# A long convolution with a gated feed-forward: real and imaginary rows in partition halves, the K spectrum moved into the middle loop, feed-forward in chunk pairs

## The chip, the cores and the metric

The kernel runs on 1 core of one Trainium2 chip. The metric is the device time of one execution in microseconds (us). The kernel before takes 271.25 us (median of 40 runs, 269.36 to 272.9). Each run is counted fast or slow; on one core, slow means only more than 1.5% above the fastest run of the same kernel. Medians and ranges below are over all runs, ratios over the fast runs alone.

Engine names as the profile has them: PE is TensorE, PEld its weight loads, DVE is VectorE, ACT is ScalarE, POOL is GpSimd, SP is SyncE.

## The reference

```python
def ref_conv(q, k, v, shift_k, ssm_k, ssm_D):        # S = 2048, D = 640
    k_pad = jnp.pad(k, ((0, 0), (3, 0), (0, 0)))
    k_shift = sum(k_pad[:, t:t + S, :] * shift_k[:, 3 - t] for t in range(4))   # four taps
    kv = k_shift * v
    # y = causal convolution of kv with ssm_k: real FFT of length 2S = 4096, product, inverse
    y = irfft(rfft(pad(kv)) * rfft(pad(ssm_k)))[:, :S, :].astype(bf16)
    return q * (y + kv * ssm_D)

x  = A_q
xn = layernorm(x)
s  = ref_conv(xn, A_k, A_v, A_shift_k, A_ssm_k, A_ssm_D)
g  = silu(gelu(xn @ w1 + b1) @ w2 + b2)              # w1 is 640 x 1728, w2 is 1728 x 640
return x + s * g
```

(shortened: casts and the generation of the inputs are left out; the factor called q inside `ref_conv` is `xn`.)

The kernel makes the transforms out of matmuls. A first stage multiplies by the sine tables `WA` and `WB` (16 units for K, the filter, and 16 for U, the shifted k times v); its results go through scratch memory in DRAM (`scrK`, `scrU`), which transposes them. A second stage multiplies by a small matrix `F2m`. The spectra are multiplied; `I1a` and `I1b` are the first half of the inverse; its result goes through `scrC`; `GA` and `GB` finish it. The two feed-forward products (FFN1 with `w1`, FFN2 with `w2`) are fed to PE between these pieces. PSUM is the on-chip memory that the matmuls write, SBUF the one that holds the other tiles. An eviction below is a copy of a matmul result out of PSUM.

## The kernel before

First stage of K (its second stage then fills `Khat`, the whole K spectrum, in SBUF):

```python
def f1_unit(rhs, scr, n2, eng, ptag):
    o_sb = ep.tile([P, 2, D], BF16, tag="o" + ptag, bufs=3, name="f1o")
    for c, W in ((0, WA), (1, WB)):
        for h in range(2):                                   # 320 columns at a time
            hs = slice(h * HALF, (h + 1) * HALF)
            ps = ps_e.tile([P, 512], F32, tag=ptag, bufs=2, name="psf1")
            nc.tensor.matmul(out=ps[:, 0:HALF], lhsT=W[:, n2, :], rhs=rhs[:, hs], ...)
            evac(..., o_sb[:, c, hs], ps[:, 0:HALF])
    nc.gpsimd.dma_start(out=sv[:, :, n2, :], in_=o_sb[:])    # to scrK or scrU

def k_unit(n2):                                              # one K unit: transposes, copy, first stage
    tp = ps_e.tile([P, 1024], BF16, tag="tp", bufs=2, name="tpk")
    for t in range(DT):
        nc.tensor.transpose(out=tp[:, t * P:(t + 1) * P], in_=kf_v[:, t, n2, :], identity=ident[:])
    kT = ep.tile([P, D], BF16, tag="kT", bufs=2, name="kT")
    nc.scalar.copy(out=kT[:], in_=tp[:, 0:D])
    f1_unit(kT, scrK, n2, "act", "f1k")

# ... cut: f2k_unit, the same with F2m, into Khat ...
kv_unit(0)
for n2 in range(NJ):
    k_unit(n2)
    emit_ffn(1)
```

The middle loop transforms U twice (the second time with swapped halves, `F2s`) and makes two products:

```python
psU  = ...  # F2m x uin   (two matmuls of 320 columns)
psUs = ...  # F2s x uin   (two more)
nc.vector.tensor_tensor(out=halves(p1[:]), in0=psU[...],  in1=halves(Khat[:, g, :]), op=ALU.mult)
nc.vector.tensor_tensor(out=halves(p2[:]), in0=psUs[...], in1=halves(Khat[:, g, :]), op=ALU.mult)
# psC = I1a x p1 + I1b x p2 ; copied to c_sb ; stored to scrC
```

## Time and profile before

| kernel | median us (range, runs) | PE busy us | PE idle us in the span | first FFN1 matmul, us |
|---|---|---|---|---|
| before | 271.25 (269.36 to 272.9, 40) | 222.4 | 46.6 | 34.6 |

The idle time is the span of the profiled execution (269.1 us) less PE's busy time.

Lines of the profile page of the kernel before. The first line is PE's busy time and share; the two strips cut the span into 40 slices of 6.7 us, each digit a busy share in tenths; then two groups of instructions (busy time and mean ns of one), and one line of the DMA issues (size, median us from issue to landing).

```profile
PE 222.4 (83%) x1424; PEld 136.0 (51%) x1437; DVE 178.3 (66%) x348; ACT 163.8 (61%) x335; POOL 49.4 (18%) x77
PE   1038689999958889999999999999998999687960
PEclk9999999999979999999999999999999999999995
...
L481 ACT CAST c_sb<-psC 128x640 bf16<-128x640 f32 x32 | 22.1, 692 | 23.2 <-PE psC L480 15.4
...
L464 PE MATMUL psUs<-uin,F2s 128*128 128x320 bf16 x64 | 13.9, 299 | 0.2
...
scrK<-f1o POOLq DMA_DIRECT2D x16, 320.0 KB, 4.4
```

The first FFN1 matmul, in the timeline of PE (start, duration, engine, line, operation):

```profile
34.59 1.24 PE L251 MATMUL ps_299<-xnT,w_sb 128*128 128x512 bf16 x4
```

PE is the limit: thin in the first five slices, then busy for nine tenths of the time or nearly so until about 230 us. `psUs` is the second transform of U, which the change removes (its 13.9 us is a sum of overlapping durations; at the pitch of 0.136 us it is 8.7 us).

The same kernel by stretches: up to the first FFN1 matmul, feed-forward beside the K and U stages, middle loop, end, and what follows. Columns: stretch and its length, busy us (and instructions) of each engine, granted TensorE clock, share of the DMA engines' time, GB/s.

```profile
0.00:34.60 34.60, 13.26 (x78) 8.07 (x79) 23.87 (x72) 17.27 (x32) 9.68 (x21) 1.00 0.92 326
34.60:157.00 122.40, 115.03 (x721) 67.94 (x728) 81.64 (x164) 101.99 (x234) 23.97 (x32) 0.99 0.55 177
157.00:224.00 67.00, 63.45 (x427) 40.98 (x432) 51.84 (x73) 35.74 (x56) 10.71 (x15) 1.00 0.52 163
224.00:260.00 36.00, 30.48 (x201) 19.02 (x199) 18.38 (x36) 8.81 (x15) 4.00 (x7) 1.00 0.70 236
260.00:270.00 10.00, 0.24 (x2) 0.00 (x0) 2.55 (x5) 0.00 (x0) 1.08 (x2) 0.61 0.16 66
```

Nearly half of PE's 46.6 us of idle time, 21.3 us, lies before the first FFN1 matmul. So the time is this start, plus PE's work after it, plus small gaps, plus a tail.

### The profile page before, as it was taken

How to read it: one execution, taken by the hardware profiler on the slowest of the kernel's cores; microseconds unless marked ns; L12 is line 12 of the kernel's file. 1: busy time of each engine (PE TensorE's matmuls, PEld its weight loads, DVE VectorE, ACT ScalarE, POOL GpSimd, SP SyncE). 2: the span in 40 equal slices, each digit the busy share in tenths (PEclk: the TensorE clock that was granted, in tenths of full speed). 3: DMA queues.
4: the chain of work that ended last, by engine and by line, in shares of the span. 5: the costliest groups of instructions: out<-in, count | busy, mean ns of one | idle time of the engine just before them, and what ended most of it. 6: DMA issues, size and time to landing. Idle time of an engine off the chain costs nothing.

```text
span 269.1 us, 4113 instructions
## 1 busy us (share of the span) xinstructions
PE 222.4 (83%) x1424; PEld 136.0 (51%) x1437; DVE 178.3 (66%) x348; ACT 163.8 (61%) x335; POOL 49.4 (18%) x77
## 2 busy tenths in 40 slices
PE   1038689999958889999999999999998999687960
PEld 0024345557635544566654456775565554454730
DVE  2785999944469899998422047349898982366770
ACT  1268499999626999974699936237664647300200
POOL 4122312342401211121112101011222222011100
PEclk9999999999979999999999999999999999999995
DMA  4999996565456565724344285214656652889721
GB/s 64 354 416 393 391 370 234 174 197 241 158 184 191 174 212 166 240 97 132 103 136 122 97 268 174 97 49 138 203 159 188 192 198 100 226 267 380 258 85 54
DMA packets 27877, 53.03 MB, mean 197 GB/s; under 512 B 5645, under 2 KB 19666, under 8 KB 27857
## 3 DMA queue, kind: packets, MB, share of 16 engines
q1 hardware_dynamic: 23056, 33.11, 40.8%
q0 software_dynamic: 4800, 19.67, 18.4%
q8 instruction: 11, 0.18, 0.3%
q14 instruction: 10, 0.07, 0.1%
HBM read 34.41 MB, written 18.36 MB: 196 GB/s over the span
## 4 chain that ended last, share of the span: by engine, by line
PE 32%; issue 24%; DMA 14%; DVE 14%; POOL 7%; ACT 6%; SPq 1%; POOLq 0%; DVEq 0%; ACTq 0%
DMA xc<-in_A_q_dram 4%; DMA w_exp<-scrW 4%; DMA uin<-scrU 3%; POOL scrC L483 3%; DVE stats L226 2%; POOL rstd L231 2%; DVE f1o L85 2%; PE psf2k L401 2%; DMA scrW<-wT_sb 2%; DVE kvtmp L410 2%; DVE uc L411 2%; DMA khc<-in_A_k_dram 2%; DVE xn L234 1%; POOL out_dram L533 1%; ACT f1o L83 1%
## 5 line engine op out<-in xcount | busy, mean ns | idle before, releaser
L262 PEld LDWEIGHTS <-hT 128*128 128x128 bf16 x448 | 44.1, 99 | 20.6 <-issue 2.3
L251 PEld LDWEIGHTS <-w_sb 128*128 128x128 bf16 x280 | 27.1, 97 | 29.7 <-issue 7.9
L481 ACT CAST c_sb<-psC 128x640 bf16<-128x640 f32 x32 | 22.1, 692 | 23.2 <-PE psC L480 15.4
L402 ACT CAST Khat<-psf2k 128x320 bf16<-128x320 f32 x64 | 25.9, 477 | 2.1 <-PE psf2k L401 2.0
L385 POOL DMA_DIRECT2D scrU<-f1o x16 | 11.0, 690 | 65.6 <-ACT f1o L83 39.3
L483 POOL DMA_DIRECT2D scrC<-c_sb x16 | 11.4, 714 | 62.5 <-ACT c_sb L481 50.7
L390 PE MATMUL tpk<-ident,Khat 128*128 128x128 bf16 x80 | 10.1, 262 | 14.3 <-DVE Khat L373 14.0
L226 DVE BATCH_NORM_STATS2 stats<-xc 128x6 f32<-128x320 bf16 x32 | 14.2, 467 | 10.9 <-DMA xc<-in_A_q_dram 10.9
L411 DVE TENSOR_TENSOR uc<-uc,kvtmp 128x1280 bf16<-128x1280 bf16 x24 | 19.6, 816 | 0.3
L410 DVE TENSOR_TENSOR kvtmp<-khc,w_exp 128x1280 bf16<-128x1280 bf16 x24 | 19.6, 817 | 0.2
L401 PE MATMUL psf2k<-kin,F2m 128*128 128x320 bf16 x64 | 16.9, 311 | 2.8 <-DMA kin<-scrK 2.8
L390 PEld LDWEIGHTS <-Khat 128*128 128x128 bf16 x80 | 9.1, 154 | 17.8 <-DVE Khat L373 14.3
L266 DVE TENSOR_TENSOR xn<-xn,sl 128x320 bf16<-128x320 bf16 x32 | 10.1, 319 | 10.9 <-ACT sl L265 10.8
L385 POOL DMA_DIRECT2D scrK<-f1o x16 | 11.1, 695 | 31.7 <-ACT f1o L83 29.9
L461 PE MATMUL psU<-uin,F2m 128*128 128x320 bf16 x64 | 14.0, 300 | 1.4 <-DMA uin<-scrU 1.2
L464 PE MATMUL psUs<-uin,F2s 128*128 128x320 bf16 x64 | 13.9, 299 | 0.2
L519 PE MATMUL psY<-cab,GA 128*128 128x320 bf16 x32 | 9.1, 300 | 5.4 <-DMA cab<-scrC 4.7
L392 ACT COPY kT<-tpk 128x640 bf16<-128x640 bf16 x16 | 12.9, 813 | 0.0
L241 ACT COPY xnT<-tpx 128x512 bf16<-128x512 bf16 x20 | 11.2, 613 | 0.2 <-PE tpx L240 0.2
L240 PE MATMUL tpx<-ident,xn 128*128 128x128 bf16 x80 | 8.7, 234 | 2.9 <-DVE xn L234 2.5
L533 POOL DMA_DIRECT2D out_dram<-o_sb x8 | 4.4, 545 | 32.7 <-DVE o_sb L531 24.6
L401 PEld LDWEIGHTS <-F2m 128*128 128x128 bf16 x64 | 6.4, 101 | 7.5 <-issue 3.0
(679 smaller groups left out, 565.5 us busy)
## 6 DMA issues: line engine op xcount, KB each, us to landing
scrK<-f1o POOLq DMA_DIRECT2D x16, 320.0 KB, 4.4
scrU<-f1o POOLq DMA_DIRECT2D x16, 320.0 KB, 2.9
kin<-scrK SPq DMA_DIRECT2D x32, 160.0 KB, 2.6
uin<-scrU SPq DMA_DIRECT2D x16, 320.0 KB, 3.3
scrC<-c_sb POOLq DMA_DIRECT2D x16, 320.0 KB, 3.8
cab<-scrC SPq DMA_DIRECT2D x16, 320.0 KB, 5.2
khc<-in_A_k_dram SPq DMA_DIRECT2D x8, 320.0 KB, 3.5
vc<-in_A_v_dram SPq DMA_DIRECT2D x8, 320.0 KB, 3.7
```

The lines of the kernel that those rows point to most:

```text
L226: nc.vector.bn_stats(out=stats[:, j, h, :], in_=xc[:, j, h * HALF:(h + 1) * HALF])
L251: nc.tensor.matmul(out=ps[:, :], lhsT=w1_sb[:, t, ft * P:(ft + 1) * P], rhs=xnT[:, t, :], start=(t == 0), stop=(t == DT - 1))
L262: nc.tensor.matmul(out=ps[:, 0:HALF], lhsT=hT[0:M, ft, q * P:(q + 1) * P], rhs=w2_sb[0:M, ft, hs], start=(ft == 0), stop=(ft == FT - 1))
L385: nc.gpsimd.dma_start(out=sv[:, :, n2, :], in_=o_sb[:])
L390: nc.tensor.transpose(out=tp[:, t * P:(t + 1) * P], in_=kf_v[:, t, n2, :], identity=ident[:])
L401: nc.tensor.matmul(out=ps[:, 0:HALF], lhsT=F2m[:], rhs=kin[:, hs], start=True, stop=True)
L402: nc.scalar.copy(out=Khat[:, g, hs], in_=ps[:, 0:HALF])
L410: nc.vector.tensor_tensor(out=tmp[:], in0=khc[:, 3 - j:KR + 3 - j, :], in1=w_exp[:, j, :, :], op=ALU.mult)
L411: nc.vector.tensor_tensor(out=uc[:], in0=uc[:], in1=tmp[:], op=ALU.add)
L461: nc.tensor.matmul(out=psU[:, h, 0:HALF], lhsT=F2m[:], rhs=uin[:, h * HALF:(h + 1) * HALF], start=True, stop=True)
L481: nc.scalar.copy(out=halves(c_sb[:, g % 2, :]), in_=psC[:, :, 0:HALF])
L483: nc.gpsimd.dma_start(out=gC[g // 2], in_=c_sb[:])
```

## The change

The intent, in the words that came with it: "Real/imaginary rows in partition halves, one U transform with a half-swapped K copy, K second stage in the middle loop, FFN in chunk pairs, x and xn resident". With real and imaginary rows in halves of the partitions, exchanging them is a copy of 64 partitions. So K is exchanged once by two DMA transfers, in place of a second transform of every U group. In addition, `GA` and `GB` are computed by DVE and ACT instead of transposed from `WA` and `WB`, all K transposes come first, evictions are 640 wide, and the U evictions, before shared by DVE and ACT, all go to ACT.

The core of the diff (much is cut; moved code is shown as it is after):

```diff
+    def kt_unit(t):                       # K transposes: ten DVE copies of 1024 in place of 16 ACT copies
+        ... 
+            nc.vector.tensor_copy(out=kT[:, h * 8:(h + 1) * 8, t * P:(t + 1) * P], in_=tp[:])
     def f1_unit(rhs, scr, n2, engs, tag):
-        o_sb = ep.tile([P, 2, D], BF16, tag="o" + ptag, bufs=3, name="f1o")
+        o = ep.tile([P, 2, D], BF16, tag="f1o", bufs=3, name="f1o")
         for c, W in ((0, WA), (1, WB)):
+            ps = ps2("psf1")
             for h in range(2):
-                ... evac(..., o_sb[:, c, hs], ps[:, 0:HALF])            # 320 wide, four a unit
+                nc.tensor.matmul(out=ps[:, h, 0:H], lhsT=W[:, n2, :], rhs=rhs[:, h * H:(h + 1) * H], ...)
+            nc.scalar.copy(out=hv(o[:, c, :]), in_=ps[:, :, 0:H])       # 640 wide, two a unit
-    build_i2_by_transpose()               # GA, GB: 32 transposes and 4 ACT copies
+    wg_pair(GA, GB, fill_g)               # GA, GB: DVE products and masks, ACT sines
...
+    for t in range(DT):
+        kt_unit(t)
+    build_small_mats()                    # F2m, I1a, I1b (each with one sine on ACT)
+    wg_pair(GA, GB, fill_g)
+    emit_ffn(1)                           # first layer norm and its transposes
+    w2_sb = big.tile([P, FT, D], BF16, tag="w2", name="w2_sb")   # takes the place of the K filter
+    nc.sync.dma_start(out=w2_sb[...], in_=B_w2[...])             # about 2.1 MB, now just ahead of:
+    load_kv(8, 4)
+    load_kv(12, 4)
+    for n2 in range(NJ):
+        f1_unit(kT[:, n2, :], scrK, n2, "aa", "k")
+        ...
+        emit_ffn(1)
...
     # middle loop
-    psUs = F2s x uin; two products of 640
+    kk[0:64, :, 1, :] = kk[64:128, :, 0, :]; kk[64:128, :, 1, :] = kk[0:64, :, 0, :]   # two DMA
+    one product of 1280: psU (broadcast) x kk
```

## The prediction

> **What bounds it now.** TensorE. The page gives PE 83% busy, DVE 66%, ACT 61%. The view by stretches shows PE thin only in 0-34 us and 230-250 us; between, it is busy 8.4 to 10 of every 10 us. In steady stretches of the timeline a 512-column matmul costs 0.216 us (five in 1.08) and a 320-column one 0.136 us (fourteen in 1.91). At these rates PE streams 60.5 us of FFN1 (280), 61 us of FFN2 (448), 69.6 us of convolution matmuls (512), and 192 transposes. FFN1 starts at 34.6 us; about 207 us of PE work and 18 us of gaps follow, to 260 us; then a 9 us tail of DVE and the last store.
>
> **What the change does.**
> 1. The swapped-U matmul goes: 64 x 0.136 = 8.7 us of PE. The 32 table transposes go: about 3 us. All critical: -11.7 us.
> 2. Evictions: K transposes move from 16 ACT copies (0.81 us) to 10 DVE copies; first- and second-stage results leave PSUM 640 wide (0.69 us, as c_sb now) instead of 320 wide (0.43-0.48). ACT falls from 164 to about 153 us, which counts only in the K stage (ACT full, 40-70 us): 3 us per K unit becomes 2.
> 3. The two products per group become one of 1280 elements. The Trainium skill ("VectorE: DVE Perf Modes", Why PSUM operands drop a tier) says an fp32 PSUM operand allows only 1x; the trace agrees (640 elements 0.82 us, pitch 0.73). One product takes about 1.45 us: no gain.
> 4. Start: shift weights no longer go through DRAM (4.9 + 10.2 us in the chain); K filter and w1 load earlier. But DVE must do both table pairs (6 + 5 us), ten K copies (12), small matrices (6) and the first layer norm (7) before FFN1, which starts at about 37-41 us, no earlier than now, but with all K transposes and most of the K first stage behind it.
> 5. Middle loop: K second stage moves in (PE 0.27, ACT 0.69 us per group), plus two half-swap DMAs per pair (5.2 MB in all). With two K buffers the loop eviction 1.6 + swap 3-4 (160 KB loads from scrK take 2.6 now) + two products 2.9 us limits a group to about 2.1-2.3 us; PE needs 1.1 us plus FFN, 1.8 in all. DMA rises from 0.5 to about 0.8 of its limit. The loop takes 70-76 us against 67 now, gaps partly filled by FFN: 5-10 us given back.
> 6. End: x and xn stay resident (three 640 KB reloads gone), C rows are 2560 contiguous bytes, so the cab waits (4.7 us on PE) shrink; stores are single rows: tail 6 us instead of 9.
>
> **Sum.** PE work after FFN1 starts is about 183 us. 39 + 183 + 18 of gaps + 6 = 246 us span, 2 us more as time: **248 us**, range 236 to 262. Faster by over 2%: 0.88; within 2%: 0.08; slower: 0.04.
>
> **What would show it.** PE busy about 208 us; F2s matmuls gone; first FFN1 matmul at 37-41 us; K first stage at 2 us a unit with ACT full; one 1.4-1.5 us product per group; swapped K halves landing in 3-4 us, and products waiting for them; middle loop 70-76 us; PE waits for cab under 2 us; last matmul to end about 6 us.
>
> **What would make it wrong.** PE's fixed order puts convolution matmuls ahead of ready FFN work while a swap DMA is in flight, so that waits reach 20 us or more; DMA saturates in the middle loop; the shared two-slot PSUM pool (U, K, first stage, Y) serialises DVE and ACT; DVE load delays FFN1 beyond 45 us. In the other direction: FFN fills every gap and FFN1 starts at 33 us, 235 us.

## The result, and the profile after

| kernel | median us (range, runs) | PE busy us | PE idle us in the span | first FFN1 matmul, us |
|---|---|---|---|---|
| before | 271.25 (269.36 to 272.9, 40) | 222.4 | 46.6 | 34.6 |
| after | 272.11 (268.04 to 274.03, 20) | 216.5 | 52.4 | 56.2 |

Ratios here are the mean time of one kernel's fast runs over that of the other's of the same rounds, so they are not quite the ratios of the medians. After over before: 0.998 (95% interval 0.995 to 1.001); with the slow runs counted in, the ratio of the means is 1.003. The change did not move the time; 248 us and the range to 262 were wrong. PE lost 5.9 us of work and gained 5.8 us of idle time.

The page of the kernel after, the same kinds of lines:

```profile
PE 216.5 (81%) x1334; PEld 130.3 (48%) x1345; DVE 167.2 (62%) x300; ACT 157.9 (59%) x253; POOL 53.1 (20%) x91
PE   1648244489989999999988979879798998888970
PEclk9999955579999999999999999999999999999996
...
L465 ACT CAST c_sb<-psC 128x640 bf16<-128x640 f32 x32 | 22.4, 700 | 17.3 <-PE psC L464 15.3
...
scrK<-f1o POOLq DMA_DIRECT2D x16, 320.0 KB, 2.5
```

The first FFN1 matmul after:

```profile
56.18 1.38 PE L324 MATMUL ps_414<-xnT,w_sb 128*128 128x512 bf16 x4
```

By stretches, with the borders at the same events (first FFN1 matmul, start and end of the middle loop, end of PE's work):

```profile
0.00:56.20 56.20, 27.76 (x156) 17.39 (x157) 40.15 (x108) 29.21 (x38) 16.21 (x32) 0.79 0.82 298
56.20:140.00 83.80, 80.36 (x503) 48.12 (x507) 56.99 (x113) 62.23 (x105) 16.83 (x27) 1.00 0.33 121
140.00:222.00 82.00, 73.47 (x435) 41.74 (x439) 46.68 (x34) 60.33 (x98) 10.73 (x15) 1.00 0.81 243
222.00:260.40 38.40, 34.81 (x246) 23.01 (x244) 22.60 (x44) 5.65 (x13) 8.82 (x16) 1.00 0.59 210
260.40:269.00 8.60, 0.14 (x2) 0.00 (x0) 0.82 (x2) 0.44 (x1) 0.54 (x1) 0.75 0.05 19
```

From the first FFN1 matmul on, PE works 188.6 us and stands for 15.6 us (the differences of lengths and busy times in the three middle rows). PE's idle time before that matmul grew from 21.3 to 28.4 us; elsewhere it did not grow. The middle loop is longer (82 us against 67), but PE is busy in 73.5 us of it. So the question is the start. In the four slices from 27 to 54 us the strip of PE, which before reads 6, 8, 9, 9, now reads 2, 4, 4, 4, and in the last three of them the clock strip reads 5.

The stretch 20 to 60 us of the kernel after, in four windows:

```profile
20.00:30.00 10.00, 8.11 (x57) 5.82 (x56) 8.69 (x39) 5.30 (x8) 2.30 (x3) 1.00 1.00 389
30.00:40.00 10.00, 3.17 (x10) 1.26 (x10) 5.79 (x19) 5.89 (x8) 2.05 (x4) 0.63 0.74 266
40.00:50.00 10.00, 3.40 (x11) 1.25 (x10) 8.57 (x23) 5.04 (x8) 3.18 (x5) 0.50 0.78 264
50.00:60.00 10.00, 8.30 (x43) 4.94 (x44) 10.00 (x22) 8.67 (x15) 1.68 (x3) 0.68 0.40 164
```

From 30 to 50 us no compute engine is full (DVE comes nearest, 8.6 of 10 us from 40 to 50); PE does a third of what it could and ACT a half. That is the picture of engines waiting for one another or for transfers, not of too much work. The DMA engines are full from 20 to 30 us. Who waits is in the timeline of ACT of the kernel after (start, duration, engine, line, operation; in brackets the idle time before it and what ended it; L266 is the first-stage eviction, L163 and L167 the `GB` and `GA` sines, L232 the sine of a small matrix, L314 the copy of the transposed layer norm):

```profile
28.30 0.69 ACT L266 CAST f1o<-psf_453 128x640 bf16<-128x640 f32 x1
29.05 0.40 ACT L232 ACTIVATE k_all<-k_all,sin_bias 128x128 f32<-128x128 int32 x1
34.11 0.69 ACT L266 CAST f1o<-psf_466 128x640 bf16<-128x640 f32 x1 [4.65 <-DMA scrK<-f1o]
34.70 0.70 ACT L266 CAST f1o<-psf_470 128x640 bf16<-128x640 f32 x1
35.28 2.01 ACT L163 ACTIVATE GB<-qT,sin_bias 128x2048 bf16<-128x2048 int32 x1
...
37.75 0.42 ACT L232 ACTIVATE k_all<-k_all,sin_bias 128x128 f32<-128x128 int32 x1
...
49.69 0.69 ACT L266 CAST f1o<-psf_582 128x640 bf16<-128x640 f32 x1 [4.63 <-DMA scrK<-f1o]
...
53.74 1.08 ACT L314 COPY xnT<-tpx 128x512 bf16<-128x512 bf16 x2
```

ACT twice stands for 4.6 us at an eviction whose buffer is still being stored. Everything ACT does after it waits too. The Trainium skill ("TensorE: Matmul & The Clock Gate", Part 1) lists ScalarE's and VectorE's instruction queues as strict FIFO; the trace agrees: the sine at 37.75 us, whose input DVE had prepared by about 33 us, comes only after three evictions (34.11, 34.70 and 37.18 us) and the `GB` sine, and DVE in turn stands behind that sine. The timeline of DVE of the kernel after shows this (L298 is the first statistics instruction of the layer norm, which FFN1 needs):

```profile
32.79 1.21 DVE L166 TENSOR_SCALAR prodT<-prodT 128x2048 int32<-128x2048 int32 x1
38.21 0.29 DVE L235 TENSOR_TENSOR I1a<-k_all 128x128 bf16<-128x128 f32 x1 [4.21 <-ACT k_all L232]
...
38.95 0.49 DVE L298 BATCH_NORM_STATS2 stats<-xreg 128x6 f32<-128x320 bf16 x1
```

The stores that it all waits for are in the chain of waits that ended last, of the kernel after:

```profile
29.29 7.01 DMA scrK<-f1o
...
43.88 7.44 DMA scrK<-f1o
```

The median store of this kind lands in 2.5 us; these two took 7.0 and 7.4. They are not the only ones: the three stores issued from 26.9 to 29.3 us took 7.0 to 7.1 us and the three from 42.4 to 45.4 us 6.9 to 7.4 us. ACT's two long waits ended with the first store of each three (issued at 26.88 and 42.41 us, landed after 7.1 and 7.2 us). All six fell beside large loads: the `w2` load (2080 KB, issued at 24.8 us, landed after 13.1 us), then the last two loads of k and one of x (640 KB each, from 41.9 us). The Trainium skill ("DMA: Bandwidth & Descriptors", Issuing engines are not separate DMA queues) says that transfers issued by different engines run on the same 16 DMA engines and interleave. The traces agree with that reading: the stores are issued by POOL and the loads by SP, and yet the stores slow down. The experiments test it. All waits of ACT for K stores in the kernel after (total, times, longest):

```profile
ACT f1o L266 <- DMA scrK<-f1o: 9.7, 3, 4.7
```

A sum suggests why the change made this visible, and the old kernel did not mind. Slow stores as such are not new: in the kernel before, the first four K stores (issued from 22.6 to 35.7 us) fell beside its own `w2` load (issued at 18.7 us, landed after 18.9 us) and took 5.8 to 6.6 us. But the K units then came 2.5 to 6.3 us apart. With three buffers, a unit's store has the length of two further units to land in. Later, in its steady stretch, units were 2.48 us apart (from the times of the store issues), so a store had 5.0 us for its median of 4.4 us, and ACT waited for a K store only once in all, 1.4 us. After the change the units that ran unhindered are 1.2 us apart (issues at 26.88, 28.10 and 29.29 us), so a store has 2.4 us, just what an undisturbed one takes. This is an estimate from the two traces: the faster first stage used up the reserve of its own buffers.

PE, kept from work, also lost its clock. The timeline of PE of the kernel after, two first-stage pairs before and one after the long wait:

```profile
29.05 0.43 PE L263 MATMUL psf_470<-xreg,WB 128*128 128x320 bf16 x2 [0.16 <-ACT f1o L266]
34.85 0.69 PE L263 MATMUL psf_494<-xreg,WA 128*128 128x320 bf16 x2 [5.37 <-ACT f1o L266]
```

The pair takes 0.69 us instead of 0.43. The Trainium skill ("TensorE: Matmul & The Clock Gate", Part 1) lists two states of the clock gate, half and all pulses, and has it at half after an idle window of about 3.4 us. The trace agrees: after a wait of 5.37 us the granted clock is 0.50 in the window 40 to 50 us. Durations show the slow rate early on too, in both kernels: a single matmul of 320 columns took 0.43 to 0.47 us in the kernel before until 32.4 us and 0.30 us at 36.8 us, and 0.45 to 0.47 us in the kernel after up to 25 us. The clock column reads 1.00 in those stretches, so it can't be relied on there.

### The profile page after: what moved, and what is told of

Same layout as the page of the kernel before. It is cut to its first block, busy times and chain, and to the rows that moved or that the text cites. A ratio compares the mean times of both kernels' runs of the same rounds, so it can differ in the third digit from the quotient of the medians.

```text
span 268.9 us, 3786 instructions
## 1 busy us (share of the span) xinstructions
PE 216.5 (81%) x1334; PEld 130.3 (48%) x1345; DVE 167.2 (62%) x300; ACT 157.9 (59%) x253; POOL 53.1 (20%) x91
## 4 chain that ended last, share of the span: by engine, by line
issue 39%; PE 29%; DMA 12%; POOL 7%; ACT 7%; DVE 4%; SPq 0%; POOLq 0%; ACTq 0%
DMA scrK<-f1o 5%; ACT f1o L266 4%; POOL scrC L467 4%; DMA kf_sb<-in_A_ssm_k_dram 3%; DMA cab<-scrC 3%; POOL out_dram L347 2%; PE tpk L249 2%; DVE prodT L166 1%; ACT xnT L314 1%; DMA scrC<-c_sb 1%; DVE xreg L250 1%; DVE prodT L177 1%; PE ps_1283 L336 1%; PE ps_1135 L336 1%; PE ps_977 L336 1%
## 5 line engine op out<-in xcount | busy, mean ns | idle before, releaser
L340 DVE TENSOR_TENSOR xreg<-xreg,sl 128x320 bf16<-128x320 bf16 x32 | 10.1, 322 | 26.6 <-ACT sl L339 26.6
L416 ACT CAST kk<-psk 128x640 bf16<-128x640 f32 x32 | 20.9, 705 | 0.0
L286 DVE TENSOR_TENSOR tmp<-k_all,w_exp 128x1280 bf16<-128x1280 bf16 x24 | 19.5, 812 | 0.1
L287 DVE TENSOR_TENSOR acc<-acc,tmp 128x1280 bf16<-128x1280 bf16 x24 | 19.5, 812 | 0.1
L414 PE MATMUL psk<-kin,F2m 128*128 128x320 bf16 x64 | 13.7, 298 | 6.6 <-DVE p_1887 L450 1.8
L495 DVE TENSOR_TENSOR xreg<-psY,xreg 128x640 bf16<-128x640 f32 x16 | 13.0, 820 | 4.4 <-PE psY L493 4.4
L347 POOL DMA_DIRECT2D out_dram<-xreg x16 | 8.6, 542 | 31.2 <-DVE xreg L346 25.8
L249 PE MATMUL tpk<-ident,kf_sb 128*128 128x128 bf16 x80 | 9.8, 309 | 6.2 <-DVE xreg L250 6.2
L298 DVE BATCH_NORM_STATS2 stats<-xreg 128x6 f32<-128x320 bf16 x32 | 14.6, 465 | 0.0
L249 PEld LDWEIGHTS <-kf_sb 128*128 128x128 bf16 x80 | 8.8, 164 | 7.5 <-issue 7.3
L314 ACT COPY xnT<-tpx 128x512 bf16<-128x512 bf16 x20 | 11.1, 599 | 0.4 <-PE tpx L313 0.4
```

The costliest lines, as they stand in the source:

```text
L249: nc.tensor.transpose(out=tp[:, q, :], in_=kf_v[:, t, h * 8 + q, :], identity=ident[:])
L286: nc.vector.tensor_tensor(out=tmp[:], in0=k_all[:, r + 3 - j:r + 3 - j + KR, :], in1=wb(j), op=ALU.mult)
L287: nc.vector.tensor_tensor(out=acc[:], in0=acc[:], in1=tmp[:], op=ALU.add)
L298: nc.vector.bn_stats(out=stats[:, j, h, :], in_=x_t[c][:, j, h * H:(h + 1) * H])
L347: nc.gpsimd.dma_start(out=out_v[:, n2, :], in_=xx)
L414: nc.tensor.matmul(out=ps[:, h, 0:H], lhsT=F2m[:], rhs=kin[:, t, h * H:(h + 1) * H], start=True, stop=True)
```

## Experiments

Three theories stood at the beginning. A: the stores of the K first stage, slow beside the big loads, hold ACT and all behind it. B: the set-up arithmetic that the change put on DVE and ACT (`GA`, `GB`, the layer norm late in DVE's order) delays FFN1 by itself. C: the start does not matter, because later stages (middle loop, end) would take any gain back. Each edit is made on the kernel after. Times are medians with their ranges, of 4 runs, and ratios to the kernel before in the same rounds (whose medians were 270.6 to 271.1 us).

### e1_f1o5: five buffers for the first-stage results

```diff
-        o = ep.tile([P, 2, D], BF16, tag="f1o", bufs=3, name="f1o")
+        o = ep.tile([P, 2, D], BF16, tag="f1o", bufs=5, name="f1o")
```

> The changed kernel with five instead of three buffers for the first-stage results; nothing else differs and the order of instructions on DVE stays the same up to the first layer norm. The changed kernel: FFN1 first matmul at 56.2 us (34.6 before), ScalarE waits 9.7 us for K stores to land. Theory A (the K stores crawl behind the w2 and k loads, ScalarE stands in order at the eviction that needs their buffer, and the sine tables, small matrices and layer norm behind it wait with it): the 9.7 us fall under 3, FFN1 starts at 46 to 51 us, the kernel is 5 to 9 us faster than before the change (262 to 266). Theory B (too much set-up arithmetic on DVE and ACT ahead of FFN1, whatever the stores do): FFN1 still starts after 54 us, time within 1.5 us of before. Theory C (the middle loop takes back whatever is gained): FFN1 earlier, time unchanged.

Measured: 262.15 us (261.91 to 264.22), ratio 0.970 (0.964 to 0.975). The first FFN1 matmul starts at 46.3 us. That is what theory A expected. ACT's waits for K stores are gone from the list of waits, though the stores are no faster (median 5.3 us): the buffers now outlast them. The windows of this run:

```profile
30.00:40.00 10.00, 4.81 (x18) 2.07 (x18) 9.79 (x32) 9.63 (x14) 4.49 (x8) 0.69 0.96 347
40.00:50.00 10.00, 8.04 (x46) 4.20 (x45) 8.97 (x21) 8.92 (x15) 3.16 (x5) 0.80 0.89 327
```

ACT is full instead of 5.9 and 5.0 of 10. The first FFN1 matmul comes 9.9 us earlier and the span is 8.6 us shorter (260.3 against 268.9), so nearly all of the gain survives to the end: this speaks for A and against C.

### e10_f1o2: two buffers, the opposite dose

```diff
-        o = ep.tile([P, 2, D], BF16, tag="f1o", bufs=3, name="f1o")
+        o = ep.tile([P, 2, D], BF16, tag="f1o", bufs=2, name="f1o")
```

> The changed kernel with two instead of three first-stage buffers: the suspected wait is made larger. Theory A: ScalarE waits for K stores to land grow from 9.7 us to 15 us or more, FFN1 starts at 60 us or later, 3 us or more slower than before the change (274 or more). Were five buffers faster for another reason (allocation, order of instructions), two buffers would cost nothing: 271 to 273 us.

Measured: 275.11 us (272.27 to 276.01), ratio 1.016 (1.009 to 1.024). The waits of ACT in this run (total, times, longest):

```profile
ACT f1o L266 <- DMA scrK<-f1o: 14.3, 4, 5.9
```

The waits follow the number of buffers: 14.3 us with two, 9.7 with three, none listed with five. The time follows in the same order, though by less than the waits grow. One expectation failed: the first FFN1 matmul is at 54.2 us, not at 60 or later, and so no later than with three buffers. In the profiled run, the fastest of the four, the span after it is 216.3 us against 212.7 with three buffers, so the loss falls after FFN1 starts; where, was not traced.

### e2_w2late and e12_loadslate: three buffers, the big loads held back

In the first, the `w2` load waits until the K first stage is over: a tiny copy from its last result into the destination keeps the load behind it. In the second, the two last loads of k are held in the same way.

```diff
-    nc.sync.dma_start(out=w2_sb[...], in_=B_w2[...])      # three transfers
-    load_kv(8, 4)                                         # e12 only
-    load_kv(12, 4)                                        # e12 only
     for n2 in range(NJ):
-        f1_unit(kT[:, n2, :], scrK, n2, "aa", "k")
+        o_k = f1_unit(kT[:, n2, :], scrK, n2, "aa", "k")
+        if n2 == NJ - 1:
+            nc.gpsimd.tensor_copy(out=w2_sb[:, :, 0], in_=o_k[:, 0, 0:FT])
+            for i in (8, 12):                             # e12 only
+                nc.gpsimd.tensor_copy(out=k_all[:, 3 + i, 0:FT], in_=o_k[:, 0, 0:FT])
+                load_kv(i, 4)
+            nc.sync.dma_start(out=w2_sb[...], in_=B_w2[...])
```

> The changed kernel with the 2 MB w2 load held back (a tiny copy from the last K result into w2 first) until the K first stage is over; three buffers as in the change. Theory A, with w2 as the traffic in the way: the first stall (ACT idle 4.65 us from 29.5 us, one store taking 7.0 us to land) is gone, stores land in under 4 us there, the second stall near 45 us (when the last k loads are on) remains; FFN1 starts at 49 to 53 us, 3 to 6 us faster than before the change. If the stores are slow for another reason (their own descriptors, the POOL queue), the first stall stays and the time does not move. Theory B: no change in time.

> The changed kernel with its three buffers for the K first-stage results, but with the feed-forward weight load and the two last K data loads all held until the K first stage is over. Theory A (the stores of the first stage are slow only because the big loads share the DMA engines with them): all stores land in 2.3 to 3.5 us, the first AND the second long wait of ScalarE are gone (sum of its waits for stores under 3 us against 9.7), the first matmul of the first feed-forward product falls from 56 to 46-50 us, time 262 to 266 us, as with five buffers, without any buffer added. Rival (three buffers are too few whatever the loads do): the waits stay at 5 us or more, first matmul 52-56 us, 267 to 272 us. A third outcome would be that the waits go but the held loads come too late, seen as PE waiting for the weights or the last K units waiting for data.

Measured: e2_w2late 267.91 us (267.16 to 269.62), ratio 0.989 (0.984 to 0.994); first FFN1 matmul at 52.8 us. The first long wait fell from 4.65 to 0.87 us; the second, 4.29 us, stayed, beside the loads of k, which had not been moved. e12_loadslate 263.24 us (262.74 to 263.37), ratio 0.973 (0.967 to 0.979); first FFN1 matmul at 49.0 us. The waits of ACT for K stores, e2_w2late first, then e12_loadslate:

```profile
ACT f1o L266 <- DMA scrK<-f1o: 5.5, 3, 4.3
```

```profile
ACT f1o L266 <- DMA scrK<-f1o: 2.6, 3, 1.5
```

Each load that is taken away takes its own wait with it, and the median store landed in 2.4 us. The expectation that all would land in 2.3 to 3.5 us failed: two took 4.0 and 5.9 us beside a load of x that now comes at 29.7 us, and the last 6.9 us beside the held `w2`. With both loads away, three buffers do almost what five do. It also speaks against the rival named in the expectation of e2_w2late, that the stores are slow by their own descriptors or their POOL queue, since those are unchanged. This is the decisive pair for A: the buffers alone could have helped for another reason (they also serve the U stage), but here no buffer was added. The third outcome, loads that come too late, does not show in the time.

### e5_gtrans: GA and GB by transposes again

One part of the change undone, for theory B: 32 transposes on PE and 4 copies on ACT, after the U first stage in the program (in the trace the first copy stands already at 27.8 us, since the order of instructions is settled when the kernel is compiled), in place of the products on DVE and the sines on ACT.

```diff
-    wg_pair(GA, GB, fill_g)
...
+    for (Gt, Wt) in ((GA, WA), (GB, WB)):
+        for q4 in range(NJ // 8):
+            tpg = ps_t.tile([P, 8, P], BF16, tag="tp", name="tpg")
+            for q in range(8):
+                nc.tensor.transpose(out=tpg[:, q, :], in_=Wt[:, q4 * 8 + q, :], identity=ident[:])
+            nc.scalar.copy(out=Gt[:, q4 * 8:(q4 + 1) * 8, :], in_=tpg[:])
```

> One part of the change undone alone: the second table pair is again made by 32 PE transposes and four ACT copies of the first pair, not computed on DVE and ACT; three first-stage buffers and everything else as in the change. Theory B (set-up arithmetic before FFN1): 5 us of DVE and 4 us of ACT sine less ahead of FFN1, so FFN1 starts 4 us or more earlier (at 52 us or before), less 3 us of added PE. Theory A (blocked evictions): the waits for K stores remain near 9 us, FFN1 starts within 3 us of 56.2, and the time is within 2 us of before the change.

Measured: 265.93 us (264.63 to 268.57), ratio 0.983 (0.977 to 0.990). The first FFN1 matmul starts at 46.4 us, yet ACT still waits 8.7 us in all for K stores (four times, 3.0 us at most). So B holds in part: with about 5 us of DVE work and two 2.0 us sines out of the way, the layer norm passes earlier although the stores are as slow. Theory A's expectation for this run, FFN1 within 3 us of 56.2, failed. It gains less than e1_f1o5 at the same FFN1 start (264.1 us of span against 260.3); PE is busy 4.7 us longer, and the K stage is still held up. A and B are two queues for the same two engines; no run has e1_f1o5 and e5_gtrans alone together, so whether their gains add is not shown.

### e3_addpool and e4_lnfirst: DVE's order

The first moves the small sum into the K filter from DVE to POOL, because DVE stands for 8 us at the beginning, waiting to do it, before it starts the tables. The second puts the layer norm of the first chunk ahead of the K transposes in the program.

```diff
-        nc.vector.tensor_tensor(out=kf_sb[:, t, 0:1], ...)      # e3_addpool
+        nc.gpsimd.tensor_tensor(out=kf_sb[:, t, 0:1], ...)
```

```diff
+    ln_unit(0)                                                  # e4_lnfirst
+    assert ffn_units.pop(0) == ("ln", 0)
     for t in range(DT):
         kt_unit(t)
```

> The changed kernel with the five tiny adds of the skip weight to the K filter on POOL instead of DVE, where four of them stand ahead of the first table and wait for filter loads until 10.0 us. Theory B (late set-up on DVE): the first table product starts near 3 us instead of 10.0, the first K eviction at 18 to 21 us instead of 25.3, FFN1 at 49 to 52 us, 4 to 7 us faster. Theory A alone: the first stage starts earlier, but its stores meet the loads earlier as well, so the waits for stores grow by about as much and FFN1 starts after 54 us; time within 2 us.

> The changed kernel with the first layer norm emitted ahead of the K transposes, so that the compile-time scheduler places it on DVE between 12 and 25 us instead of 39 to 48 us. If the layer norm is what FFN1 waits for: FFN1 starts at 42 to 46 us, 8 to 12 us faster. Theory A: the evictions of the transposed x and the second table pair still stand behind the blocked K evictions on ScalarE, FFN1 starts at 48 us or later, at most 5 us faster.

Measured: e3_addpool 272.18 us (269.9 to 272.96), ratio 1.003 (0.997 to 1.009): nothing, as against the 4 to 7 us of theory B. The first K eviction came at 25.1 us (25.3 without the edit), because DVE then waited 6.8 us for the K transposes, and the waits for stores were 9.5 us. e4_lnfirst 267.0 us (266.7 to 268.01), ratio 0.986 (0.982 to 0.989): the first FFN1 matmul starts at 29.3 us, before any other version, earlier than either expectation had it, but FFN1 breaks off from 32 to 43 us: ACT stands 3.4 us at a store, then has evictions and the `GB` sine to do, and the first Gelu comes at 42.2 us; the next ones come at 47.8 us, after the last large sine at 44.2 us. The expectation of e7_f1o5_lnfirst below puts this down to FFN1's output tile, which shares two buffers with the scratch of the table work; no run tests that. So an early first matmul is not the same as an early FFN1.

### e7_f1o5_lnfirst and e6_all3: the parts together

```diff
+ bufs=5 as in e1_f1o5, ln_unit(0) first as in e4_lnfirst          # e7_f1o5_lnfirst
+ the same, and GA, GB by transposes as in e5_gtrans               # e6_all3
```

> Five first-stage buffers and the layer norm first, the second table pair computed as in the change. FFN1 starts near 29 us as with the layer norm alone, but its output tile shares its two slots with the table scratch, so the first Gelu has to wait for the last table sine (at about 36 us instead of 44, since ScalarE is no longer blocked). Expected 256 to 261 us: better than either part alone (262.2 and 267.0).

> Five first-stage buffers, the first layer norm emitted first, and the second table pair by transposes, together. If the late start was the whole error of the prediction, its own sum holds with the real start: FFN1 at 29 to 33 us with no long break after it, and 248 us or less. If the later stages take back the gain (theory C): FFN1 as early, but above 256 us.

Measured: e7_f1o5_lnfirst 261.61 us (260.99 to 264.9), ratio 0.969 (0.961 to 0.978); e6_all3 263.55 us (262.62 to 265.46), ratio 0.974 (0.969 to 0.980). The gains of these parts do not add: neither beats e1_f1o5 clearly, e7_f1o5_lnfirst misses the expected 256 to 261 us narrowly, and e6_all3 the 248 us by far. By its time alone e6_all3 is the outcome for theory C (FFN1 at 30.3 us, but above 256 us). The timeline of ACT in e6_all3 shows one thing that took the gain back, at the start and not in the later stages (L232 is the sine of a small matrix, L326 the Gelu of FFN1):

```profile
33.82 0.69 ACT L326 ACTIVATE hT<-ps,b_f 128x512 bf16<-128x512 f32 x1
34.52 1.28 ACT L232 ACT_TABLE_LOAD   x1
35.82 0.40 ACT L232 ACTIVATE k_all<-k_all,sin_bias 128x128 f32<-128x128 int32 x1
...
36.82 1.28 ACT L326 ACT_TABLE_LOAD   x1
38.11 0.69 ACT L326 ACTIVATE hT<-ps,b_f 128x512 bf16<-128x512 f32 x1
```

FFN1 now runs among the last sines, and each change between Sin and Gelu costs a load of ACT's function table: seven loads of 1.28 us between 32.5 and 47.9 us, 9.0 us in all. How much of the time that explains, no run of its own shows.

### e9_setup and e11_setup_gfirst: all sines ahead of the first Gelu

Five buffers and the sum on POOL. In addition the small matrices are built before the K transposes. In e9_setup the layer norm then comes before the `GA`, `GB` work, in e11_setup_gfirst after it.

```diff
+ bufs=5 (e1_f1o5), the sum on POOL (e3_addpool)
+    build_small_mats()
     for t in range(DT):
         kt_unit(t)
-    build_small_mats()
+    ln_unit(0)                                       # e9_setup only
+    assert ffn_units.pop(0) == ("ln", 0)             # e9_setup only
```

> Five first-stage buffers, the five small adds on POOL, the small matrices emitted ahead of the K transposes (DVE is idle there for filter loads until 10 us in the change) and the layer norm ahead of the second table pair; all sines come before the first Gelu, so that one table load is left where the layer-norm-first kernels had three to seven. If the set-up order is what is left of the error: first K eviction at 20 to 23 us, FFN1 from 35 to 39 us without a break, 252 to 257 us, clearly under the 262.2 of five buffers alone. If stages after FFN1 starts take the gain back: 260 us or more.

> As e9_setup, but the second table pair stays ahead of the layer norm as in the change. FFN1 waits for the layer norm, which comes 4 to 5 us later on DVE: FFN1 at 39 to 43 us, 1 to 4 us slower than e9_setup. If FFN1 waits for something else (w1, the table sines), the two are equal within 1 us.

Measured: e9_setup 258.86 us (254.38 to 261.45), ratio 0.948 (0.938 to 0.959), first FFN1 matmul at 36.6 us; e11_setup_gfirst 258.0 us (255.31 to 258.91), ratio 0.953 (0.945 to 0.962), first matmul at 39.7 us. No difference can be told: FFN1 starts 3 us later in e11_setup_gfirst, but the four runs of e9_setup spread over 7 us, more than the 1 to 4 us that were in question. Which of the parts of these two versions brings the gain over e1_f1o5 was not separated either. The timeline of ACT in e9_setup:

```profile
22.52 6.13 ACT L266 CAST f1o<-psf 128x640 bf16<-128x640 f32 x10 [2.56 <-PE psf L263]
30.47 1.95 ACT L266 CAST f1o<-psf 128x640 bf16<-128x640 f32 x3 [1.81 <-DMA scrK<-f1o]
32.31 2.01 ACT L163 ACTIVATE GB<-qT,sin_bias 128x2048 bf16<-128x2048 int32 x1
...
37.21 2.00 ACT L167 ACTIVATE GA<-prodT,sin_bias_p 128x2048 bf16<-128x2048 int32 x1
39.23 1.28 ACT L326 ACT_TABLE_LOAD   x1
40.53 1.27 ACT L326 ACTIVATE hT<-ps,b_f 128x512 bf16<-128x512 f32 x2
```

There is one table load, and one short wait for a store. These are the best versions, and both beat both kernels. In e9_setup's profiled run PE works 212.4 us and is idle for 40.2 us of a span of 252.6 us; the prediction had 208 of work in a span of 246, so 38 idle. This profiled run is the fastest of the four. The spread of e9_setup over its four runs is 7 us, more than that of any other version; its cause stays open.

### e8_kk3: three K buffers in the middle loop

The prediction took the two K buffers for the limit of the middle loop.

```diff
-        kk = midp.tile([P, 2, 2, D], BF16, tag="kk", bufs=2, name="kk")
+        kk = midp.tile([P, 2, 2, D], BF16, tag="kk", bufs=3, name="kk")
```

> The changed kernel with three instead of two buffers for the second-stage K of the middle loop. If the loop is limited by refilling two K buffers (eviction, swap DMAs, two products), as the prediction had it: the loop from the first product (144 us) to the last scrC store (222 us) shortens by 5 us or more, time 3 to 6 us down. If PE and its fixed order with FFN limit it: loop and time within 1.5 us of the change as it is (271 to 272).

Measured: 271.48 us (270.32 to 274.7), ratio 1.001 (0.997 to 1.006), nothing. In the profiled run the last store to `scrC` was issued at 218.9 us against 222.1, so the loop may be 3 us shorter, less than the 5 us expected, and the time did not follow. The number of K buffers does not set the time. DVE's waits for the swapped halves exist (11.2 us the first time in the kernel after, when the loop starts; 11.3 here), but PE has feed-forward work meanwhile.

## Why the prediction was wrong

The predicted sum was 39 (start of FFN1) + 183 (PE work after it) + 18 (gaps) + 6 (tail) = 246 us of span. The trace has 56.2 + 188.6 + 15.6 + 8.6 = 269.0.

1. **The step that failed is step 4, "Start": "FFN1, which starts at about 37-41 us".** It started at 56.2 us, which is 17 of the 23 us of error (PE's work adds 5.6 and the tail 2.6; the gaps give back 2.4). The step added up DVE's work only. It left out that the K first stage, which it rightly made faster, would overrun three buffers when its stores were slowed to 7 us by the loads beside them; and that ACT and DVE work in order, so that a blocked eviction blocks the sines and the layer norm behind it. PE stands in order too: the normalised x was ready at 48.6 us, but its transposes came at 50.9 us, behind a first-stage matmul that waited for the second blocked eviction. Left out as well were 8.3 us at the beginning in which DVE waits for loads; e3_addpool shows that taking this wait off DVE alone gains nothing. Holding the loads (e12_loadslate) brings the start to 49.0 us, more buffers (e1_f1o5) to 46.3 us, and a better order of the set-up with them (e9_setup) to 36.6 us. The predicted start could be had, but not from this program. The prediction's risk "DVE load delays FFN1 beyond 45 us" named the right event and only a part of the cause: from 30 to 40 us DVE was busy for only 5.8 of 10 us, waiting for ACT, though e5_gtrans, with less set-up work on DVE and ACT, also brings the start to 46.4 us.
2. **The K stage.** Predicted: "K first stage at 2 us a unit with ACT full". ACT was busy 5.9 and 5.0 of 10 us instead; it was 9.6 and 8.9 when the buffers sufficed (e1_f1o5). Unhindered units took 1.2 us, better than predicted, and that was part of the trouble.
3. **PE's work.** The removals are real: no `psUs` matmul is left. But of the predicted saving of 11.7 us PE's busy time shows 5.9. PE ran at half clock for much of 30 to 60 us. An estimate from the durations: at the slow rate matmuls of 320 columns in a row come about 0.13 us further apart (0.26 us against 0.136) and transposes about 0.05 us (0.11 against 0.06); the kernel before has 30 and 55 slow ones, the kernel after 42 and 100, e9_setup 14 and 79. That makes 6.7, 10.7 and 6.6 us of extra work, so the half clock would be about 4 of the 5.8 us that are missing, and about all of the 4.1 us by which e9_setup (212.4 us of PE work) is below 216.5. No run separates it from the rest, and the prediction's 208 us was reached by no version.
4. **Copies.** The ten K copies on DVE cost 0.68 us each, not 1.2 us: a small error in the safe direction. The Trainium skill ("VectorE: DVE Perf Modes", Why PSUM operands drop a tier) allows bf16 data from PSUM twice the rate of fp32, which I had not applied; a copy of 1024 bf16 elements in 0.68 us against a product with 640 fp32 ones in 0.82 us agrees.
5. **The product of 1280** took 1.49 us against a predicted 1.45, with fp32 in PSUM: right, and no gain.
6. **Middle loop.** Predicted 70 to 76 us, measured about 82, at a DMA share of 0.81 (predicted 0.8). PE's idle time in it was 8.5 us, within the predicted 5 to 10 us of "given back". The mechanism named, two K buffers and swaps of 3 to 4 us, is right about the swap (3.2 us) and wrong about its consequence: e8_kk3 shows no effect of a third buffer on the time.
7. **End.** The `cab` waits of PE were 3.5 us, not under 2 (4.7 before); the tail was 8.6 us, not 6.

Shown by experiments: that the loads slow the stores (e2_w2late, e12_loadslate), that this and the amount and order of the set-up work held the time at 272 (e1_f1o5, e10_f1o2, e5_gtrans, e9_setup), and that the later stages keep most of a gain made at the start (e1_f1o5, e12_loadslate, e9_setup). Only argued from traces: how much of PE's extra busy time is the half clock, why the tail did not shrink, and that the reserve of two unit lengths was what shielded the kernel before. Open: the spread of e9_setup, and where two buffers lose their time.

## What to carry to other kernels

When a stage is made faster, work out again how long its output buffers cover a store (buffers minus one, times the new unit length) and compare that with a store beside the loads of that moment, not with a store alone. When an in-order engine evicts results and also computes tables, look at what stands behind each eviction, because one late store then delays chains that have nothing to do with it. Sum up a start-up phase along its waits and not along one engine's work.

## What the Trainium skill lacked or had wrong

- "DMA: Bandwidth & Descriptors" says that transfers of all issuing engines interleave on the same 16 DMA engines, but the section cited gives no figure of what that does to a small transfer. Here a store of 320 KB took 2.4 us undisturbed, 7.0 to 7.1 us beside a load of 2080 KB and 6.9 to 7.4 us beside loads of 640 KB.
- "ScalarE: Activation LUTs", What ACT_TABLE_LOAD costs, has about 1283 ns for the load, which agrees with 1.28 us here, plus about 1380 ns of drain for every switch. No such drain shows here: in e6_all3 the load starts at 34.52 us, just after the Gelu of 33.82 to 34.51 us, and the sine starts at 35.82 us, so a switch took 1.3 us.
- I found no page that joins the strict order of an engine's queue to the reuse of buffers: here a store that landed 4.7 us late (7.1 us against 2.4) held ACT's sines, through them DVE's layer norm, and through that the first feed-forward matmul.
